# Three row blocks of the first batch transposed by DMA, and the turns behind the first batch set anew

## The chip, the cores and the metric

The kernel runs on one core of a Trainium2 chip. The metric is device time in microseconds. A core has TensorE (PE, with its weight loads PEld), VectorE (DVE), ScalarE (ACT), GpSimd (POOL), and SyncE (SP), which here only issues DMAs. Each of them works off its own instructions in order. Sixteen DMA engines move the data; the loads, the outputs and the DMA transposes are all issued on SP's queue, the MLP's weights on POOL's.

## The reference

Two stages run one after the other, on 4 batches, 8 heads, 768 positions and 64 channels a head. The first is a retention recurrence; the second mixes its output by a Fourier transform over positions and channels, normalizes, and applies an MLP of width 2048.

```python
for t in range(S):
    state = gamma[None, :, None, None] * state + einsum('bhd,bhe->bhde', k[:, :, t], v[:, :, t])
    y[:, :, t] = scale * einsum('bhd,bhde->bhe', q[:, :, t], state)
x = y.transpose(0, 2, 1, 3).reshape(B, S, H * D)          # 4 x 768 x 512
u = x + real(fft(fft(x, axis=1), axis=2))
un = (u - mean(u)) / sqrt(var(u) + 1e-6)                  # over the 512 channels
out = u + maximum(un @ w_ch1, 0) @ w_ch2
```

## The kernel before, in words

**Retention.** The 768 positions are cut into 6 chunks of 128, and the heads are taken in 4 pairs (called 0 to 3 in their order). For a pair, `cast_unit` turns the loaded float32 q, k and v into float16 on POOL (L428, L438, L443), `t_unit` makes the transposes qT and kT, `kv_unit` the chunk states (L683, L693), `a_unit` the scores inside the chunks (PE L664, then DVE's masked product L667), and `y_unit` the output (PE L714, L718, then ACT L726 into the tile x). For the second batch q and k are transposed on TensorE (L620), but kT of pairs 2 and 3 by DMA (L616). The third and fourth batch transpose both by DMA (L609, L611).

**Fourier mixing.** `fold_s`, `fold_d`, `fold_e` fold x by its symmetries on DVE, `s1_unit` is the transform over positions (L847), `s2_unit` that over channels, one row block of 128 positions at a time (PE L1009 or, for the first batch, L1025 and L1028; then ACT, DVE, and POOL L1037 and L1039, which write the tile u). `norm_unit` takes mean and variance on DVE (L1049, L1050) and writes the centred float16 row block `un` on ACT (L1051).

**MLP.** Each row block `un` is transposed into `unT` by `unT_unit`: either by four TensorE transposes into PSUM (L1074) and an eviction by DVE (L1076) or ACT (L1078), or by one DMA transpose on SP's queue (L1070). Before the change row blocks 3 to 5 of the second batch and all blocks of the third and fourth go by DMA; the first batch's and the second batch's blocks 0 to 2 go over TensorE. `h_unit` is the first matmul over 384 positions, in 16 units of four matmuls (L1087, evicted by ACT L1091 or DVE L1093); the first batch's first half is done by row block instead (`h0_unit`, L1104). `ch_unit` is the second matmul (L1130), in four parts of four matmuls for each row block, with the output's sum on DVE (L1134) and its DMA (L1138).

**Order.** The first batch's retention and mixing up to its third row block stand in a list written out by hand (`FIRST`), and every engine's order is pinned to it. Everything behind that is in streams: a stream is a list of units with a first and a last turn, and its units are spread evenly between the two (`emit`). One unit of turn is one batch of MLP: the first batch's MLP has 56 units in its "majors" stream, from turn 0 to 1, and the attention of batch b + 1 and the mixing run beside it. All units are emitted in the order of their turns. That order is a priority: a scheduler in the compiler then takes, on each engine, the unit that is ready and has the earliest turn, so units can be pulled forward where an engine would stand idle. Only POOL's order is kept as emitted (`pin`).

The turns that the change touches: `DM0` (first batch's row blocks 3 to 5: mixing between its first two numbers, transposes between its last two), `TS0` (second batch's casts and the five steps of its attention), `DA0` (second batch's transform over positions, then the mixing and transposes of its row blocks 0 to 2, counted from the end of the attention), `LD0` (the second batch's loads, L195) and `HT0` (`half_tables`, small tables for the folded transform, and `pad_unit`, zeros in the q tiles). The second batch's loads also wait for the seventh of the eight weight DMAs (`load_unit` with `after`), since both draw on the same DMA engines.

Of the kernel before, what the change touches and what calls it, by code (L numbers as in the profile page):

```python
# [12 lines left out]
ALU = mybir.AluOpType  # L13
# [44 lines left out]
ACT_ROWS = ((2, 5, 6, 7, 8, 9, 10, 14), (0, 3, 6, 7, 9, 10, 11, 12, 14, 15), (2, 4, 5, 6, 7, 8, 10, 11, 13, 14))  # L58


@with_exitstack
def kernel(
# [9 lines left out]
    nc = tc.nc  # L72
# [112 lines left out]
    def load_unit(b, i, after=None, names="qkv"):  # L185
        def run():
            h0 = 2 * PAIR_ORDER[i]
            for name in names:
                if (name, b, i) in in_of:
                    continue  # L190
                src = srcs[name]
                t = inp.tile([P, 2, NCH, D], f32, tag="in32", name=f"{name}32")
                rows = "h (p c) d -> p h c d" if b < NPE and name == "q" else \
# [13 lines left out]
                in_of[name, b, i] = t  # L207
        return run
# [34 lines left out]
    for h in range(H):  # L243
# [52 lines left out]
    def pad_unit():  # L296
        for j in range(2):
            nc.vector.memset(qzs[j][:, 0, :, D:P], 0.0)
            nc.vector.memset(qzs[j][:, 1, :, 0:D], 0.0)

# [115 lines left out]
    def cast_unit(b, i):  # L416
        def run():
            h0 = 2 * PAIR_ORDER[i]
            q32, k32, v32 = (in_of.pop((n, b, i)) for n in "qkv")
            kd = kp.tile([P, NCH, 2, D], f16, tag="kd16", name="kd16")  # L420
            v16 = vp.tile([P, NCH, 2, D], f16, tag="v16", name="v16")
            with ExitStack() as es:
                if b < NPE:
                    if (b, i - 1) in last_cast:
                        es.enter_context(tc.issue_after(last_cast[b, i - 1].ins))
                    q16 = qzs[i % 2].rearrange("p h c d -> p (h c d)")[
                        :, 0:NCH * P].rearrange("p (c h d) -> p c h d", c=NCH, h=2)
                    es.enter_context(tc.issue_after(nc.gpsimd.tensor_scalar(  # L428
                        out=q16, in0=q32.rearrange("p h c d -> p c h d"), scalar1=1.0,
                        scalar2=1.0, op0=ALU.mult, op1=ALU.mult).ins))  # L430
                else:
                    q16 = qzs[i % 2]
                    for h2 in range(2):
                        dst = q16[:, h2, :, D * h2:D * h2 + D]
                        nc.gpsimd.tensor_scalar(out=dst, in0=q32[:, h2], scalar1=1.0,
                                                scalar2=1.0, op0=ALU.mult, op1=ALU.mult)
                for h2 in range(2):
                    kc = nc.gpsimd.tensor_scalar(out=kd[:, :, h2, :], in0=k32[:, h2],  # L438
                                                 scalar1=gkd[:, h0 + h2:h0 + h2 + 1],
                                                 scalar2=1.0, op0=ALU.mult, op1=ALU.mult)  # L440
# [162 lines left out]
    def t_unit(b, i):  # L603
        def run():
# [9 lines left out]
            for dst, src in ((qT, q16_of[b, i]), (kT, kd_of[b, i])):  # L614
                if dst is kT and i in KD:
                    nc.sync.dma_start_transpose(kT, src.rearrange("p c h d -> p (c h d)"))  # L616
                    continue
                tq = ps_g.tile([P, NCH, P], f16, tag="g", name="tq", padded_shape=[P, 8, P])
                for c in range(NCH):
                    nc.tensor.transpose(tq[:, c, :], src[:, c].rearrange("p a b -> p (a b)"),  # L620
                                        ident16)
                if dst is qT:
                    for h2 in range(2 if b else 1):
                        rows = slice(D * h2, D * h2 + D) if b else slice(0, P)
                        dst = qT[rows, h2] if b else qT
                        (nc.scalar.copy if h2 == 0 or ON_ACT["q"][min(b, 2)] else nc.vector.tensor_copy)(
                            dst.rearrange("p c t -> p (c t)").rearrange(
                                "p (t c) -> p t c", c=NCH),
                            tq[rows].rearrange("p c t -> p t c"))
                else:  # L630
                    nc.scalar.copy(dst, tq)
# [434 lines left out]
    def unT_unit(b, kb):  # L1066
        def run():
            un, unT = lb[b].pop(("un", kb)), lb[b]["unT"]
            if b > 1 or b and kb >= 3:
                nc.sync.dma_start_transpose(unT[:, :, kb * P:(kb + 1) * P], un)  # L1070
                return
            pst = ps_g.tile([P, 4, P], f16, tag="g", name="pst", padded_shape=[P, 8, P])
# [84 lines left out]
    def attn_steps(b):  # L1157
        steps = []
        for step in range(6):
            un = []  # L1160
            if step < 4:
                un.append(held(cast_unit(b, step)))
            i = step - 1
            if 0 <= i < 4:
                un.append(kv_unit(b, i))
            i = step - 2
# [175 lines left out]
```

## Time and profile before

| | |
|---|---|
| median of 3 runs | 242.59 us (241.97 to 243.15) |
| the profiled execution's own time | 242.18 us |
| its span, first to last instruction | 240.4 us |
| granted TensorE clock | 1.00 |
| busy: PE, DVE, ACT, POOL | 228.3, 173.4, 120.8, 82.8 us |
| first matmul of the first batch's MLP (L1104) | 32.5 us |
| first h unit of its second half (L1087) | 60.3 us |
| first matmul of the second batch's MLP (L1087) | 91.0 us |

All times in the profile are of one execution, counted from its span's start. A line of a group reads: code line, engine, operation, what it writes and reads, how many, busy time, mean duration of one in ns, and the engine's idle time ahead of them with what ended it. In a timeline a line gives start, duration, engine, code line, operation and count, with neighbours of one kind merged; matmuls are pipelined, so a matmul's duration is longer than the step to the next one, and what a matmul costs is that step. "SPq" is SP issuing a DMA, and the time of an issue includes waiting for room in the queue.

### The profile page before, as it was taken

What the parts mean: (1) busy time and instruction counts of PE and PEld (TensorE: products, weight loads), DVE (VectorE), ACT (ScalarE), POOL (GpSimd) and SP (SyncE); (2) the same over time, 40 slices, a digit from 0 to 9 for tenths busy, and PEclk for the clock granted to TensorE, in tenths of its full rate; (3) what the DMA queues carried; (4) which work ended last, traced back from release to release, by engine and by line L of the source; (5) the groups of instructions that cost most, each with busy time, mean ns of one, the idle gap of its engine ahead of it and who ended that gap; (6) DMA issues with size and microseconds to landing.
All of it is one profiled execution on the core that took longest, in us unless ns stands there. A gap on an engine that the chain in (4) does not pass through costs nothing.

```text
span 240.4 us, 5243 instructions
## 1 busy us (share of the span) xinstructions
PE 228.3 (95%) x1999; PEld 142.5 (59%) x1999; DVE 173.4 (72%) x421; ACT 120.8 (50%) x268; POOL 82.8 (34%) x151
## 2 busy tenths in 40 slices
PE   0988999999999999999999999999999999999994
PEld 0466779766774756665567446655675455446542
DVE  8999887958898789977895749977886557215121
ACT  5989758675864544931148406722366227203400
POOL 7678802675300197840002808920004124000000
PEclk9999999999999999999999999999999999999999
DMA  7999999999999289979999488675100331221012
GB/s 181 231 271 238 236 206 208 215 248 246 260 215 230 47 197 218 179 144 146 256 277 208 103 174 213 131 109 153 46 0 0 90 109 24 43 90 45 0 44 87
DMA packets 100808, 36.77 MB, mean 153 GB/s; under 512 B 91440, under 2 KB 97840, under 8 KB 100784
## 3 DMA queue, kind: packets, MB, share of 16 engines
q1 hardware_dynamic: 96560, 32.25, 63.2%
q0 software_dynamic: 4224, 4.19, 10.5%
q8 instruction: 15, 0.25, 0.5%
q14 instruction: 9, 0.07, 0.1%
HBM read 27.26 MB, written 6.29 MB: 140 GB/s over the span
## 4 chain that ended last, share of the span: by engine, by line
PE 85%; DVE 4%; DMA 3%; POOL 2%; ACT 2%; SPq 1%; issue 1%; ACTq 0%
PE psc L1130 34%; PE psh L1087 28%; PE psh L1104 3%; PE wkA L664 3%; DMA v<-in_v_dram 3%; PE ps L847 3%; PE wkY L718 2%; PE pq L1009 2%; PE ps L827 1%; PE wkY L714 1%; PE wkK L683 1%; PE pq L921 1%; SPq L215 1%; PE tq L620 1%; POOL q16z L453 1%
## 5 line engine op out<-in xcount | busy, mean ns | idle before, releaser
L1130 PE MATMUL psc<-w,ht 128*128 128x512 f16 (+2 forms) x400 | 88.9, 370 | 0.0
L1087 PE MATMUL psh<-unT,w 128*128 128x384 f16 x448 | 81.6, 326 | 0.3 <-ACT ht L1091 0.3
L1130 PEld LDWEIGHTS <-ht 128*128 128x128 f16 x400 | 37.6, 98 | 36.7
L1087 PEld LDWEIGHTS <-w 128*128 128x128 f16 x448 | 42.1, 98 | 24.2 <-issue 0.8
L1091 ACT ACTIVATE ht<-psh 128x384 f16<-128x384 f32 x66 | 31.7, 490 | 41.2 <-PE psh L1087 40.6
L1037 POOL TENSOR_TENSOR u<-u,x 128x256 f32<-128x256 f32 x21 | 13.3, 635 | 107.8 <-DVE u L1016 95.6
L1134 DVE SCALAR_TENSOR_TENSOR ob<-psc,stats,u 128x512 f32<-128x512 f32 (+2 forms) x25 | 18.1, 725 | 29.2 <-PE psc L1130 29.0
L1093 DVE TENSOR_SCALAR ht<-psh 128x384 f16<-128x384 f32 x46 | 25.3, 550 | 8.9 <-PE psh L1087 8.4
L667 DVE TENSOR_TENSOR atm<-wkA,maskp 128x512 f16<-128x512 f32 x36 | 23.6, 681 | 1.5 <-PE wkA L664 1.5
L1051 ACT ACTIVATE un<-u,stats 128x512 f16<-128x512 f32 x21 | 14.9, 719 | 12.2 <-DVE stats L1050 8.2
L1049 DVE BATCH_NORM_STATS2 bst<-u 128x6 f32<-128x512 f32 x21 | 14.5, 688 | 4.9 <-POOL u L1039 4.7
L693 DVE SCALAR_TENSOR_TENSOR s<-s,gk,wkK 128x128 f16<-128x128 f16 x48 | 16.2, 337 | 2.4 <-ACT s L689 1.6
L726 ACT ACTIVATE x<-wkY,gexp 128x384 f16<-128x384 f32 x24 | 12.9, 581 | 9.0 <-PE wkY L718 8.9
L438 POOL TENSOR_SCALAR kd<-k,gexp 128x384 f16<-128x384 f32 x24 | 13.8, 586 | 3.3 <-DMA k<-in_k_dram 3.1
L664 PE MATMUL wkA<-qTz,kT 128*128 128x256 f16 x72 | 13.2, 272 | 0.1
L1039 POOL TENSOR_TENSOR u<-u,x 128x256 f32<-128x256 f32 x21 | 13.3, 635 | 0.0
L1011 ACT COPY qn<-pq 128x128 f32<-128x128 f32 x18 | 4.9, 274 | 13.7 <-PE pq L1009 13.7
L1104 PEld LDWEIGHTS <-w 128*128 128x128 f16 x192 | 11.0, 98 | 0.9 <-issue 0.6
L1104 PE MATMUL psh<-unT,w 128*128 128x128 f16 x192 | 11.4, 219 | 0.1
L1016 DVE SCALAR_TENSOR_TENSOR u<-pq,g,qn 128x256 f32<-128x256 f32 x18 | 8.5, 474 | 3.2 <-PE psh L1087 2.5
L443 POOL TENSOR_SCALAR v<-v 128x768 f16<-128x768 f32 x12 | 10.0, 832 | 1.6 <-DMA v<-in_v_dram 1.6
L664 PEld LDWEIGHTS <-kT 128*128 128x128 f16 x72 | 6.9, 98 | 5.7 <-issue 0.6
(177 smaller groups left out, 311.9 us busy)
## 6 DMA issues: line engine op xcount, KB each, us to landing
q<-in_q_dram SPq DMA_DIRECT2D x16, 384.0 KB, 6.1
k<-in_k_dram SPq DMA_DIRECT2D x16, 384.0 KB, 5.4
v<-in_v_dram SPq DMA_DIRECT2D x16, 384.0 KB, 6.0
out_dram<-ob SPq DMA_DIRECT2D x23, 256.0 KB, 2.4
w<-in_moe_w_ch_dram POOLq DMA_DIRECT2D x8, 512.0 KB, 10.9
unT<-un SPq DMA_TRANSPOSE x15, 2.4
out_dram<-ob SPq DMA_DIRECT2D x1, 192.0 KB, 1.9
kT<-kd SPq DMA_TRANSPOSE x10, 3.0
```

The source lines that it names most:

```text
L438: kc = nc.gpsimd.tensor_scalar(out=kd[:, :, h2, :], in0=k32[:, h2], scalar1=gkd[:, h0 + h2:h0 + h2 + 1], scalar2=1.0, op0=ALU.mult, op1=AL ...
L664: mm = nc.tensor.matmul(wk[:, c2], st["kT"][:, c, :], st["qT"][:, :, c, :], start=True, stop=True)
L667: nc.vector.tensor_tensor(out=st["atm"][:, 2 * part:2 * part + 2], in0=wk, in1=maskp[:, PAIR_ORDER[i]].unsqueeze(1).to_broadcast([P, 2, 2, ...
L693: nc.vector.scalar_tensor_tensor(out=s16[:, c], in0=s16[:, c - 1], scalar=gk2[:, hp:hp + 1], in1=wk[:, c - c0], op0=ALU.mult, op1=ALU.add)
L1049: nc.vector.bn_stats(bst, u[:, kb, :])
L1051: nc.scalar.activation(un, u[:, kb, :], AF.Identity, bias=stats[:, kb, 0:1], scale=-1.0)
L1087: nc.tensor.matmul(psh, w116[:, cb, fb * P:(fb + 1) * P], unT[:, cb, rt * 384:(rt + 1) * 384], start=(cb == 0), stop=(cb == 3))
L1091: nc.scalar.activation(ht16[:, fb, :], psh, AF.Relu, bias=0.0, scale=-1.0)
L1093: nc.vector.tensor_scalar(out=ht16[:, fb, :], in0=psh, scalar1=-1.0, scalar2=0.0, op0=ALU.mult, op1=ALU.max)
L1104: mm = nc.tensor.matmul(psh[:, f], w116[:, cb, fb * P:(fb + 1) * P], unT[:, cb, kb * P:(kb + 1) * P], start=(cb == 0), stop=(cb == 3))
L1130: nc.tensor.matmul(psc[:, c0:c1], ht16[:, fb, rb3 * P:(rb3 + 1) * P], w216[:, fb, c0:c1], start=(fb == 0), stop=(fb == NFB - 1))
L1134: nc.vector.scalar_tensor_tensor(out=ob[:, c0:c1], in0=psc[:, c0:c1], scalar=lb[b]["st"][:, rb, 3:4], in1=lb[b]["u"][:, rb, c0:c1], op0=AL ...
```

## The change

Row blocks 3, 4 and 5 of the first batch are transposed by a DMA on SP's queue in place of TensorE and an eviction; the table `UD` says which blocks of the first two batches do so. All turns of the streams behind the first batch's list, up to the second batch's first three row blocks, get new numbers. `QD`, a way to transpose q by DMA as well, is added but empty, so what it guards is as before.

```diff
-DM0, DM1 = (0.183, 0.205, 0.286, 0.408), (0.004, 0.137, 0.232, 0.341)
-TS0 = (0.228, 0.358, 0.398, 0.465, 0.512, 0.573, 0.684, 0.694)
+DM0, DM1 = (0.079, 0.166, 0.238, 0.282), (0.004, 0.137, 0.232, 0.341)
+TS0 = (0.335, 0.390, 0.418, 0.440, 0.525, 0.605, 0.703, 0.726)
 TS1 = (-0.040, -0.020, 0.048, 0.585)
-DA0, DA1 = (0.043, 0.161, 0.176, 0.190, 0.284, 0.321), (0.063, 0.067, 0.063, 0.158, 0.168, 0.189)
-LD0, LD1 = (0.223, 0.312), (-0.370, 0.140)
-HT0 = (0.666, 0.693, 0.632, 0.590)
+DA0, DA1 = (0.013, 0.146, 0.137, 0.188, 0.260, 0.288), (0.063, 0.067, 0.063, 0.158, 0.168, 0.189)
+LD0, LD1 = (0.142, 0.375), (-0.370, 0.140)
+HT0 = (0.712, 0.769, 0.606, 0.689)
 NPE = 2
 KD = (2, 3)
+QD = ()
 NT = 0.6
+UD = ((3,4,5), (3, 4, 5))
...
             un, unT = lb[b].pop(("un", kb)), lb[b]["unT"]
-            if b > 1 or b and kb >= 3:
+            if b > 1 or kb in UD[b]:
                 nc.sync.dma_start_transpose(unT[:, :, kb * P:(kb + 1) * P], un)
                 return
```

Turns of some units before and after:

| unit | before | after |
|---|---|---|
| mixing of the first batch's blocks 3, 4, 5 | 0.190, 0.198, 0.205 | 0.108, 0.137, 0.166 |
| their transposes | 0.327, 0.367, 0.408 | 0.253, 0.267, 0.282 |
| second batch's loads, pairs 0 to 3 | 0.245, 0.268, 0.290, 0.312 | 0.200, 0.259, 0.317, 0.375 |
| its casts, pairs 0 to 3 | 0.293, 0.409, 0.472, 0.521 | 0.363, 0.422, 0.452, 0.536 |
| scores of pair 2 (three parts) | 0.556 to 0.573 | 0.582 to 0.605 |
| y of pair 3 | 0.686 | 0.707 |
| second batch's transform over positions | 0.766 to 0.855 | 0.772 to 0.872 |
| its mixing of blocks 0, 1, 2 | 0.875, 0.879, 0.884 | 0.880, 0.897, 0.914 |
| their transposes | 0.990, 1.003, 1.015 | 0.995, 1.005, 1.014 |

More of the change, by code (lines that the diff above doesn't have):

```diff
@@ L192, in run @@
                 t = inp.tile([P, 2, NCH, D], f32, tag="in32", name=f"{name}32")
-                rows = "h (p c) d -> p h c d" if b < NPE and name == "q" else \
+                rows = "h (p c) d -> p h c d" if b < NPE and name == "q" and i not in QD else \
                     "h (c p) d -> p h c d"
@@ L294, in half_tables, with pad_unit @@
                                 scalar2=1.0, op0=ALU.mult, op1=ALU.mult)
-    def pad_unit():
-        for j in range(2):
+    def pad_unit(js=None):
+        for j in (js if js is not None else {0, 1} - {i % 2 for i in QD}):
             nc.vector.memset(qzs[j][:, 0, :, D:P], 0.0)
@@ L422, in run @@
             with ExitStack() as es:
-                if b < NPE:
-                    if (b, i - 1) in last_cast:
-                        es.enter_context(tc.issue_after(last_cast[b, i - 1].ins))
+                if b < NPE and (b, i - 1) in last_cast:
+                    es.enter_context(tc.issue_after(last_cast[b, i - 1].ins))
+                if b < NPE and i not in QD:
                     q16 = qzs[i % 2].rearrange("p h c d -> p (h c d)")[
@@ L616, in run @@
                     nc.sync.dma_start_transpose(kT, src.rearrange("p c h d -> p (c h d)"))
+                    continue
+                if dst is qT and i in QD:
+                    nc.sync.dma_start_transpose(qT.rearrange("p h c t -> p (h c) t"),
+                                                src.rearrange("p h c d -> p (h c d)"))
                     continue
@@ L1161, in attn_steps @@
             if step < 4:
+                if b == 1 and step in QD:
+                    un.append(lambda j=step % 2: pad_unit([j]))
                 un.append(held(cast_unit(b, step)))
```

6 lines of the change are left out of this document (4 added, 2 removed).

## The prediction

> **What bounds the kernel now.** I read the page's busy shares and its chain first, then the windows, the tile views of the transposes, the timelines and the waits of the stage that is changed.
>
> ```profile
> PE 228.3 (95%) x1999; PEld 142.5 (59%) x1999; DVE 173.4 (72%) x421; ACT 120.8 (50%) x268; POOL 82.8 (34%) x151
> PE 85%; DVE 4%; DMA 3%; POOL 2%; ACT 2%; SPq 1%; issue 1%; ACTq 0%
> ```
>
> TensorE is busy for 95% of the span and carries 85% of the chain. Time is won here only by taking work off TensorE or by closing its few gaps. The windows (PE, PEld, DVE, ACT, POOL, then clock, DMA share, GB/s) show this in the stage that is changed:
>
> ```profile
> 44.00:48.00 4.00, 4.00 (x42) 2.67 (x40) 3.65 (x11) 3.05 (x5) 2.64 (x5) 1.00 1.10 235
> 56.00:60.00 4.00, 4.00 (x49) 2.66 (x47) 3.28 (x7) 2.33 (x5) 2.07 (x3) 1.00 1.22 249
> 72.00:76.00 4.00, 4.00 (x34) 2.11 (x33) 3.14 (x7) 2.49 (x7) 0.00 (x0) 1.00 1.17 236
> ```
>
> PE is full, the granted clock is 1.00, and the DMA engines are full too (share above 1). So a transpose taken off PE frees time there and costs time in a stream that is already saturated. The tile view of the PSUM tile of the transposes, and the line view of the DMA transposes that later batches use already:
>
> ```profile
> L1074 PE MATMUL pst<-ident,un x32: 219/219/219, 35.3 to 90.1; 128*128 128x128 f16 x32
> L1076 DVE COPY unT<-pst x4: 411/416/426, 37.4 to 90.5; 128x512 f16<-128x512 f16 x4
> L1078 ACT COPY unT<-pst x4: 564/579/586, 38.7 to 90.1; 128x512 f16<-128x512 f16 x4
> ...
> L1070 SPq DMA_TRANSPOSE unT<-un x15: 1188/1216/2628, 98.5 to 204.8; - x15
> ...
> DMA to landing us min/median/max: 2.3/2.4/4.8
> ```
>
> The PE timeline shows what a row block's four transposes hold up, and the first use of the third pair's kT:
>
> ```profile
> 48.08 0.39 PE L1074 MATMUL pst<-ident,un 128*128 128x128 f16 x4
> 48.31 1.89 PE L1130 MATMUL psc<-w,ht 128*128 128x512 f16 x8
> ...
> 63.91 2.11 PE L1087 MATMUL psh<-unT,w 128*128 128x384 f16 x12
> 65.86 0.82 PE L664 MATMUL wkA<-qTz,kT 128*128 128x256 f16 x6
> ```
>
> The next matmul starts 0.23 us after the four. Of SP's and POOL's timelines, the end of the second batch's loads:
>
> ```profile
> 56.33 4.16 SPq L1138 DMA_DIRECT2D out_dram<-ob  x3
> 60.65 1.35 SPq L616 DMA_TRANSPOSE kT<-kd  x1
> ...
> 58.92 0.83 POOL L428 TENSOR_SCALAR q16z<-q 128x768 f16<-128x768 f32 x1 [1.17 <-DMA q<-in_q_dram]
> 60.56 1.15 POOL L438 TENSOR_SCALAR kd<-k,gexp 128x384 f16<-128x384 f32 x2 [0.82 <-DMA k<-in_k_dram]
> ```
>
> The casts wait for loads that land some 1.7 us apart (46.9 for the first k to 61.6 for the last v, ten loads). The third pair's kT is issued behind three outputs at 60.65 and lands at 64.47.
>
> **Transposes off TensorE.** Three row blocks (3, 4, 5) by four transposes. The price is the step to the next instruction, not the row's 219 ns: 0.224 us for four, so 3 x 0.224 = **-0.67 us** on the path, as PE has no gap at these places. ACT loses two evictions (2 x 0.58) and DVE one (0.42); neither is on the path there (both idle over a microsecond between 50 and 54), so nothing. The Trainium skill, TensorE: Matmul & The Clock Gate, Part 4, gives about 275 ns for such a transpose inside a kernel. By that, as an estimate, twelve would free 3.3 us; the trace's 56 ns steps decide against it.
>
> **Three DMA transposes on SP.** Each takes 1.2 us of SP's time and 2.4 us to land, 4.8 at worst. The last `un` (block 5) is written on ACT by 47.2, its first user is the second half's first matmul at 60.27, 0.67 earlier after the change: even behind a full stream, at the loads' 6.1 us, it lands by about 55. Nothing on the path. What they delay is the queue behind them: the loads of pairs 2 and 3 (L195), the outputs (L1138) and the kT transposes (L616). In the DMA stream a block is 128 KB where a load is 384 KB per 1.7 us, so 0.57 us each, 1.7 in all. SP's own time bounds it from above, 3 x 1.2 = 3.6 us, if nothing of it overlaps; the lower bound is nothing. I take 1.7, since SP already waits for room in its queue there (a load's issue takes 0.4 to 2.4 us). Slack on the other side: pair 3's q cast is done at 59.8 and transposed at 63.6 (3.8 us), its v cast at 62.5 and used at 66.5 (4.0): covered. The third pair's kT has 65.86 - 64.47 = 1.4 us, the thinnest cover.
>
> **Turns set anew.** One turn is from 32.5 to 91.0 us, 58.5 us; one unit of the 56 is 0.018. They decide who goes first among what is ready, so half_tables and pad (already pulled to DVE's free time at 47.6 to 50.7) stay free, as do the batch's own mix units: their PE part already runs at 36.9 in a gap, and POOL keeps its order. Load 3 now stands behind the first output (turn 0.375 against 0.339), 0.65 us of stream at the spacing at which the outputs land; pair 3's 3.8 us cover it. The second batch's casts and attention move later by 0.01 to 0.07; its third pair's scores go behind one more h unit (0.65 us), so they are due at 65.86 + 0.65 - 0.67 = 65.8, and kT, 1.7 us late, lands at 66.2: 0.3 us, which a ready h unit hides if the order has one there, as it has now (two of them go ahead of the scores). I take 0. In the stage's gaps,
>
> ```profile
> PE ps L891 <- DVE xg L882: 0.2, 1, 0.2
> ```
>
> is the only one that counts as a wait; all steps lengthened by over 60 ns between 35 and 91 us come to 1.3 us. I see no reason why the new turns close them all or open others: between -1.3 and the prices below, I take 0.
>
> **Sum.** The profiled execution took 242.18 us (span 240.4 and 1.8 around it): 242.18 - 0.67 = 241.5. It lies 0.41 under the median 242.59 of the three runs; against the median, 242.59 - 0.67 = **241.9 us**, by itself too little to be told from no change (0.5%, 1.2 us, is about what can be told).
>
> **Rivals.** (1) The new turns also close the gaps: up to 1.3 us more, 240.6 to 241.3. For it: the waits of the second batch's y units on DVE's score products sit among what is moved. Against: they come from DVE, which is solid from 65.4 to 74.1, and little leaves it.
>
> (2) Slower: the third pair's kT comes late. Place: L664's wait for L616. With SP's whole 3.6 us, kT lands at 68.1, PE, due at 65.8, stands 2.3 us: 242.59 - 0.67 + 2.3 = 244.2. It decides for slower from a stall of 1.9 us, kT landing after 67.7, 3.2 us later than now. For it: SP is a queue in order, an output now stands ahead of the last load, and each transpose waits there for its `un`. Against: the stream's own price is half of that, and h units can go first.
>
> (3) The seam to the second batch eats the gain. The chain of waits around it:
>
> ```profile
> 74.41 1.06 ACT x L726 x2
> ...
> 89.84 0.45 PE pst L1074 x8
> 90.28 0.23 PE pq L1009 x4
> 90.51 0.28 PE wkK L683 x5
> 90.79 0.33 PE pq L1009 x4
> 91.13 3.95 PE psh L1087 x24
> ```
>
> From the last y (74.4) through folds, DFT and norm to the new unT it takes 16.7 us; meanwhile PE works off the first batch's rest and, at its end, 0.8 us of pulled-forward work. The two arrive together. If the chain does not start earlier, PE's 0.67 us turns into waiting: 242.6. If the last y comes later as its turn says (0.686 to 0.707, 1.2 us), 243.8. Against: DVE has 0.7 us of outputs between the last norms' steps that another order can put behind them.
>
> (4) A transpose costs its whole row: 12 x 0.219 = 2.6 us, 240.0. The timeline's steps speak against it. It is the trace's nearest to the page's 275 ns.
>
> **How the numbers follow.** The forecast, 241.4 to 242.6, 0.36. Rival 1: 0.20. Rival 2: 0.28, of which 0.22 beyond its point. Rival 3: 0.14, of which 0.04 slower by over 0.5% (a little behind 243.8). Rival 4: 0.02. Faster 0.20 + 0.02 = 0.22; same 0.36 + 0.06 + 0.10 = 0.52; slower 0.22 + 0.04 = 0.26. The predicted time is the forecast's, 241.9; the range goes from rival 1's end, 240.6, to rival 2's, 244.3.
>
> **What would show it.** L1074 with 20 matmuls in place of 32 and L1070 with 18 issues; PE's work before the first matmul of the second batch's h units less by 0.67 us. That matmul at 90.3 means the forecast, at 91.0 rival 3, later than 91.5 a new stall. A wait of L664 for kT, with L616 landing after 66.5, is rival 2; casts waiting for loads after 64 us would mean that the stream is delayed by more than 1.7 us. A gap ahead of L1087 near 59 to 60 us, released by a DMA, would mean that the transposes themselves come late, which I left out. The stage after 91 us should be as long as before; if it isn't, the later batches' loads were pushed, and the forecast is wrong there.

## The result, and the profile after

The changed kernel takes 243.96 us (median of six runs, 243.67 to 244.56) against 242.33 us for the kernel before in the same comparison (six runs, 241.97 to 243.15): a ratio of **1.0066, 95% interval 1.0044 to 1.0088**. It is slower by 1.6 us. The profiled execution took 244.01 us, its span is 242.0 us, 1.6 us longer than before. The forecast was 241.9 us and "no change". The time lies inside the range given, near its upper end, but not by the mechanism that put that end there.

The page's busy shares and chain of the changed kernel:

```profile
PE 227.3 (94%) x1987; PEld 141.6 (59%) x1987; DVE 173.6 (72%) x420; ACT 119.7 (49%) x266; POOL 82.9 (34%) x151
...
PE 78%; DVE 6%; DMA 6%; POOL 3%; ACT 3%; issue 2%; SPq 1%; ACTq 0%; DVEq 0%
```

TensorE has twelve matmuls and 1.0 us of work less, as meant, and yet the span is longer. The chain says where to look: TensorE's share of it fell from 85% to 78%, and that of DMA rose from 3% to 6%. The tile views of the transposes (code lines have moved: L1074 is now L1082, L1070 is L1078) show the change itself:

```profile
L1082 PE MATMUL pst<-ident,un x20: 219/219/230, 35.7 to 90.4; 128*128 128x128 f16 x20
```

```profile
L1078 SPq DMA_TRANSPOSE unT<-un x18: 1189/1216/2137, 45.1 to 206.6; - x18
...
DMA to landing us min/median/max: 2.3/2.4/4.8
```

And of the table of waits of the changed kernel (engine, tile, line, what it waited for: total us, times, longest):

```profile
PE wkA L672 <- DMA qTz<-q16z: 1.5, 1, 1.5
...
PE pst L1082 <- ACT un L1059: 0.3, 1, 0.3
```

Neither is in the table of before. The second is at the seam to the second batch; the first is far behind everything that the change touches. The span cut into stages shows the same (us; a stage goes from one first matmul to the next, the batches' ones being those of their h units):

| stage | before | after | difference |
|---|---|---|---|
| start to the first batch's MLP (L1104, now L1112) | 32.50 | 32.90 | +0.40 |
| from there to the second batch's MLP | 58.52 | 58.43 | -0.09 |
| second batch's MLP to the third's | 51.28 | 52.77 | **+1.49** |
| third to fourth | 51.68 | 51.66 | -0.02 |
| fourth to the end | 46.40 | 46.25 | -0.15 |

The 0.40 us of the first row are not the change's: over the fourteen profiles of this study, whose list for the first batch is one and the same, it took between 32.45 and 33.03 us, whichever kernel it was. So two things need an explanation: the 0.67 us taken off TensorE brought 0.09 in their own stage, and the stage behind, in which no turn was changed, lost 1.49 us.

**The stage behind.** There the third batch's last pair waits for its qT. TensorE's timeline in the changed kernel, and then the chain of waits around it (start, duration, what):

```profile
113.81 2.54 PE L1138 MATMUL psc<-w,ht 128*128 128x512 f16 x11
117.83 0.38 PE L672 MATMUL wkA<-qTz,kT 128*128 128x256 f16 x2 [1.48 <-DMA qTz<-q16z]
```

```profile
110.98 6.71 DMA qTz<-q16z
117.70 0.14 issue
117.83 0.38 PE wkA L672 x2
```

Counted as steps from one matmul to the next, TensorE loses 1.65 us here. In the kernel before it lost 0.30 at the same matmul. TensorE reaches these scores 24.85 us behind the second batch's first h unit in both kernels; the transposed q lands 25.02 us behind that unit before the change, and 26.37 us after it. SP's timeline shows the order in which it is issued. Before:

```profile
92.86 0.43 SPq L195 DMA_DIRECT2D k<-in_k_dram  x1
...
97.95 0.39 SPq L195 DMA_DIRECT2D v<-in_v_dram  x1
98.45 2.63 SPq L1070 DMA_TRANSPOSE unT<-un  x1
101.40 1.21 SPq L611 DMA_TRANSPOSE kT<-kd  x1
102.66 1.51 SPq L609 DMA_TRANSPOSE qTz<-q16z  x1
104.27 2.82 SPq L1070 DMA_TRANSPOSE unT<-un  x2
107.26 1.21 SPq L611 DMA_TRANSPOSE kT<-kd  x1
108.52 0.57 SPq L195 DMA_DIRECT2D q<-in_q_dram  x1
109.19 4.14 SPq L609 DMA_TRANSPOSE qTz<-q16z  x1
```

And after:

```profile
93.26 0.43 SPq L197 DMA_DIRECT2D q<-in_q_dram  x1
...
97.78 0.57 SPq L197 DMA_DIRECT2D k<-in_k_dram  x1
98.40 0.71 SPq L197 DMA_DIRECT2D v<-in_v_dram  x1
101.74 1.42 SPq L615 DMA_TRANSPOSE kT<-kd  x1
103.20 1.49 SPq L613 DMA_TRANSPOSE qTz<-q16z  x1
104.79 4.15 SPq L1078 DMA_TRANSPOSE unT<-un  x3
109.04 1.23 SPq L615 DMA_TRANSPOSE kT<-kd  x1
110.32 0.57 SPq L197 DMA_DIRECT2D q<-in_q_dram  x1
110.98 2.67 SPq L613 DMA_TRANSPOSE qTz<-q16z  x1
```

The same transfers stand in another order. Before, the third batch's last q load went out ahead of all of this (at 83.82), and one of the second batch's unT transposes filled the time that SP spent waiting for the casts. After, that q load comes at 93.26, the k and v loads behind it side by side at 97.78 and 98.40, SP stands idle from 99.1 to 101.7, and all three unT transposes come behind kT and qT of the third pair. So the issue of the last qT begins 1.47 us later behind the second batch's first h unit (19.65 against 18.18), and it lands 1.35 us later. SP is done with that issue 22.3 us behind the unit in both kernels, so its later start alone doesn't make the landing late. That the landing hangs on SP's order is what the runs below show; by which step it does is not shown.

**The changed stage.** I count each of TensorE's steps at the usual step of its shape (0.16 us for 384 columns, 0.215 for 512), and what a step has above that as loss. From the first batch's first MLP matmul to the second batch's, the usual steps come to 55.38 us before and 54.74 after, 0.64 less; the losses come to 3.14 before and 3.69 after, 0.55 more. Almost all of the latter is one wait, at 90.27, for the centred row block of the second batch:

```profile
89.55 0.40 PE L1082 MATMUL pst<-ident,un 128*128 128x128 f16 x4
90.27 0.40 PE L1082 MATMUL pst<-ident,un 128*128 128x128 f16 x4 [0.33 <-ACT un L1059]
```

The last y of the second batch ends 42.44 us behind the stage's start (41.93 before), its last `un` 57.31 (56.89). Why that y is later can be counted. Ahead of the third pair's scores TensorE takes 20 matmuls of h units, where it took 12 before:

```profile
64.30 3.41 PE L1095 MATMUL psh<-unT,w 128*128 128x384 f16 x20
67.55 0.82 PE L672 MATMUL wkA<-qTz,kT 128*128 128x256 f16 x6
```

With these eight, 63 of the 64 h matmuls of the first batch's second half stand ahead of the last y, where 55 did. Eight steps are 1.3 us more ahead of it, the twelve transposes 0.64 less, and the y comes 0.51 later. From its end to the second batch's first h unit it takes 15.99 us (16.58 before, when nine h matmuls were left for that stretch; now one is). So what came off TensorE ahead of the y was more than filled by work pulled forward, and the chain behind the y came later.

### The profile page after: what moved, and what is told of

It reads as the page before. It is cut to its first block, busy times and chain, and to the rows that moved or that the text cites. A ratio compares the mean times of both kernels' runs of the same rounds, so it can differ in the third digit from the quotient of the medians.

```text
span 242.0 us, 5220 instructions
## 1 busy us (share of the span) xinstructions
PE 227.3 (94%) x1987; PEld 141.6 (59%) x1987; DVE 173.6 (72%) x420; ACT 119.7 (49%) x266; POOL 82.9 (34%) x151
## 4 chain that ended last, share of the span: by engine, by line
PE 78%; DVE 6%; DMA 6%; POOL 3%; ACT 3%; issue 2%; SPq 1%; ACTq 0%; DVEq 0%
PE psc L1138 29%; PE psh L1095 29%; PE psh L1112 3%; PE wkA L672 3%; DMA v<-in_v_dram 3%; DMA qTz<-q16z 3%; PE ps L855 3%; PE wkY L726 2%; PE pq L1017 1%; PE wkY L722 1%; PE wkK L691 1%; SPq L217 1%; PE ps L835 1%; PE tq L628 1%; POOL u L1047 1%
## 5 line engine op out<-in xcount | busy, mean ns | idle before, releaser
L1112 PEld LDWEIGHTS <-w 128*128 128x128 f16 x192 | 11.0, 98 | 0.8 <-issue 0.5
L1112 PE MATMUL psh<-unT,w 128*128 128x128 f16 x192 | 11.4, 219 | 0.1
```

What stands on the lines that cost most here:

```text
L1112: mm = nc.tensor.matmul(psh[:, f], w116[:, cb, fb * P:(fb + 1) * P], unT[:, cb, kb * P:(kb + 1) * P], start=(cb == 0), stop=(cb == 3))
```

## The experiments

In the edits, `order on SP` is a dependency that only fixes the order of two DMAs on SP's queue: the first argument is issued behind the second. No semaphore and no wait is added. In the changed kernel and in its four runs that reorder only the entries on SP near the second and third batch, the orders on TensorE, VectorE, ScalarE and GpSimd are the same, instruction by instruction; so they are in the kernel before and its two such runs. The experiments of the last part and those with other turns have orders of their own. "Stage A" is from the first batch's first MLP matmul to the second batch's (58.52 us before, 58.43 after), "stage B" from there to the third batch's (51.28 and 52.77). A stage, a wait or a landing is that of the one execution profiled; four of these took 0.8 to 1.6 us more than the median of their run (the DMA transposes alone, unT and the q load both moved, the earlier kT, the old DM0), so their waits may be longer than usual.

### One half of the change at a time

Only the DMA transposes, all turns as before:

```diff
+UD = ((3,4,5), (3, 4, 5))
...
-            if b > 1 or b and kb >= 3:
+            if b > 1 or kb in UD[b]:
```

> The old turns with the three DMA transposes alone. Theory (SP's order in the second batch): the change's 1.6 us come from one transpose of the second batch (row block 3) that now stands behind the third batch's transposes of pair 2 on SP; here it stands ahead of them again, so TensorE's wait ahead of the last pair's scores (L672) should be 0.3 us as in the kernel before and the time 241.7 to 242.5 us. Rival (the DMA transposes themselves cost): about 243.9 us, as in the changed kernel.

Measured: 246.81 us (246.34 to 247.83), ratio 1.0173 (1.0149 to 1.0197). Stage A takes 64.38 us, stage B 51.14. SP's timeline and TensorE's waits:

```profile
55.35 1.48 SPq L197 DMA_DIRECT2D v<-in_v_dram  x1
56.92 4.29 SPq L1078 DMA_TRANSPOSE unT<-un  x1
61.31 0.52 SPq L1146 DMA_DIRECT2D out_dram<-ob  x1
61.92 2.53 SPq L1078 DMA_TRANSPOSE unT<-un  x2
```

```profile
PE psh L1095 <- DMA unT<-un: 3.0, 1, 3.0
PE wkY L722 <- ACT qTz L634: 0.6, 1, 0.6
```

Neither of the expected times came. With the old turns the transposes stand behind all of the second batch's loads, land at 63.1, 64.4 and 65.7 us, and the second half of the MLP waits until 65.85. The step that the prediction put at nothing is worth over 3 us when its cover is gone. And there is no wait at the third batch's last qT (it lands 24.52 us behind the second batch's first h unit): the DMA transposes by themselves do not cause it.

Only the new turns, all transposes of the first batch on TensorE, as an edit to the changed kernel:

```diff
-UD = ((3,4,5), (3, 4, 5))
+UD = ((), (3, 4, 5))
```

> The new turns with all of the first batch's transposes on TensorE. Theory (SP's order in the second batch): row block 3's transpose stands ahead as in the kernel before, so a wait of 0.3 us at L672 and 242.0 to 242.9 us. Rival (the new turns alone are slow, whatever is transposed where): 243.5 us or more, 0.67 us above the changed kernel if TensorE's transposes cost as before.

Measured: 243.58 us, ratio 1.0043 (1.0029 to 1.0058). Stage A takes 59.78 us, stage B 51.57. TensorE's waits:

```profile
PE pst L1082 <- ACT un L1059: 1.0, 2, 0.8
...
PE wkA L672 <- DMA qTz<-q16z: 0.4, 1, 0.4
```

The rival's time, 243.5 us or more, held. The new turns alone cost 0.4%, most of it in the changed stage. The TensorE transposes now come ahead of their `un` (a step loss of 0.98 us at 46.80), the seam has a wait of 0.40 us with or without DMA transposes, and the third batch's last qT is late by 0.57 us. The halves do not add up (1.7% and 0.4% against 0.7%): the turns are made for the DMA transposes.

### Which part of SP's order makes the last qT late

Three orders, each with the unT transpose of the second batch's row block 3 moved. First the changed kernel with that transpose ahead of the third pair's kT, as before the change:

```diff
-                nc.sync.dma_start_transpose(unT[:, :, kb * P:(kb + 1) * P], un)
+                x = nc.sync.dma_start_transpose(unT[:, :, kb * P:(kb + 1) * P], un).ins
+                if (b, kb) == (1, 3):
+                    tc.add_manual_dep(sp_of["k", 2, 2], x.name, mybir.DependencyInfo(mybir.DependencyClass.NoSync, mybir.DependencyReason.DATA), reason="order on SP")
```

> The changed kernel with one edge: the third batch's kT of pair 2 is issued behind the second batch's row block 3 on SP, as in the kernel before. Theory (SP's order): the wait at L672 falls from 1.65 to about 0.3 us, the stage from the second to the third batch's first h unit from 52.8 to 51.4 us, the time to 242.3 to 242.7 us. Rivals (transposes or turns in the first batch): no change, 243.9 us.

Measured: 243.58 us, ratio 1.0045 (1.0029 to 1.0062). The step loss falls from 1.65 to 1.24 us only. The moved transpose holds SP for 3.73 us, as it is issued directly behind the k and v loads (2.63 us in the kernel before, which has the k load earlier).

Then the kernel before, with the same transpose behind the third pair's kT and qT, as after the change:

```diff
+                if (b, kb) == (1, 3):
+                    tc.add_manual_dep(x, sp_of["k", 2, 2].name, mybir.DependencyInfo(mybir.DependencyClass.NoSync, mybir.DependencyReason.DATA), reason="order on SP")
+                    tc.add_manual_dep(x, sp_of["q", 2, 2].name, mybir.DependencyInfo(mybir.DependencyClass.NoSync, mybir.DependencyReason.DATA), reason="order on SP")
```

> The kernel before with the opposite edge: the second batch's row block 3 is transposed behind the third batch's kT and qT of pair 2 on SP, as in the changed kernel. Theory (SP's order): SP reaches the last qT 1.25 us later, the wait ahead of the last pair's scores (L664) grows from 0.3 to some 1.5 us, the time to 243.4 to 243.9 us. Rivals: no change, 242.3 us.

Measured: 243.08 us, ratio 1.0033 (1.0015 to 1.0051). The loss rises from 0.30 to 0.79 us: half a microsecond, less than the 1.2 expected, by an edit to the kernel before that touches nothing of the first batch. Both runs say that this transpose's place is a part of the cause, worth 0.4 to 0.5 us, and that there is more.

Last, the changed kernel with that and with the third batch's last q load ahead of its first qT:

```diff
+                if (name, b, i) == ("q", 2, 3):
+                    tc.add_manual_dep(sp_of["q", 2, 0], dma.ins.name, mybir.DependencyInfo(mybir.DependencyClass.NoSync, mybir.DependencyReason.DATA), reason="order on SP")
```

> The changed kernel with both shifts on SP undone: the third batch's last q load is issued ahead of its first qT (as in the kernel before), and the second batch's row block 3 is transposed ahead of the third batch's pair 2. Undoing the second alone left a wait of 1.24 us. Theory (what is left is the load that had moved into the seam, 384 KB in the same stream): the last qT lands about 25.0 to 25.3 us after the second batch's first h unit, as before, the wait is 0.2 to 0.5 us, the time 242.3 to 242.8 us. Rival (the seam is slow for another reason, such as the second batch's later loads): the wait stays at 1.2 us or more, 243.5 us.

Measured: 243.24 us (242.24 to 245.05), ratio 1.0043 (1.0016 to 1.0069), and a loss of 1.88 us in an execution of 244.43; the 0.2 to 0.5 expected was missed. The k and v loads still stood side by side (97.52 and 98.14), and the transpose behind them held SP for 4.15 us. Moving single entries did not bring the order of before back.

### The load ahead of the last qT

In both kernels the fourth batch's first q load is issued just ahead of the late qT. It is wanted much later. Behind it:

```diff
+                if (b, i) == (3, 0):
+                    tc.add_manual_dep(dma.ins, sp_of["q", 2, 3].name, mybir.DependencyInfo(mybir.DependencyClass.NoSync, mybir.DependencyReason.DATA), reason="order on SP")
```

In the changed kernel:

> The changed kernel with one edit: the fourth batch's first q load is issued on SP behind the third batch's last qT (in the kernel it stands directly ahead of it). Theory (the 1.65 us wait is the landing of that qT, and the load ahead of it is part of the price): a qT behind no load lands some 3.8 us after its issue in place of 6.7 us, so it is there 3 us earlier, the wait at L672 is gone, the stage from the second to the third batch's first h unit is 51.1 us and the time 242.1 to 242.5 us. Rival (the wait is set by something else than this landing, such as the cast or TensorE's own use of the buffer): 243.9 us.

Measured: 242.19 us, before 242.34, ratio 0.9998 (0.9980 to 1.0016). The wait is gone, stage B takes 51.14 us. SP and TensorE there:

```profile
109.17 1.23 SPq L618 DMA_TRANSPOSE kT<-kd  x1
110.49 1.30 SPq L615 DMA_TRANSPOSE qTz<-q16z  x1
111.84 1.02 SPq L197 DMA_DIRECT2D q<-in_q_dram  x1
```

```profile
113.61 2.75 PE L1142 MATMUL psc<-w,ht 128*128 128x512 f16 x12
116.20 0.38 PE L676 MATMUL wkA<-qTz,kT 128*128 128x256 f16 x2
```

The transpose lands 5.4 us behind its issue in place of 6.7, and no longer waits 0.66 us for the load's issue. One moved load takes the whole loss away; the rest of SP's order is that of the changed kernel.

In the kernel before, the same edit:

> The kernel before with the same edit (the fourth batch's first q load behind the third batch's last qT). Theory: its 0.3 us wait at L664 goes, 241.9 to 242.3 us, at most 0.2% faster. Rival (the load is needed early, in the fourth batch): a new wait in the third stage, slower than 242.6 us.

Measured: 241.89 us, ratio 0.998 (0.997 to 0.999). The 0.30 us that the kernel before lost here go too. This version is the fastest of the study and beats both kernels, by little.

### SP's order of before, with the change otherwise whole

The changed kernel, with the order on SP behind the first batch set to that of before, entry by entry (the last q and k load of the third batch, the second pair's qT ahead of its kT, the third pair's the other way, and unT as above), the late q load left where it is in both:

```diff
+                if (name, b, i) == ("q", 2, 3):
+                    tc.add_manual_dep(sp_of["q", 2, 0], dma.ins.name, mybir.DependencyInfo(mybir.DependencyClass.NoSync, mybir.DependencyReason.DATA), reason="order on SP")
+                if (name, b, i) == ("k", 2, 3):
+                    tc.add_manual_dep(sp_of["q", 2, 1], dma.ins.name, mybir.DependencyInfo(mybir.DependencyClass.NoSync, mybir.DependencyReason.DATA), reason="order on SP")
...
+                if (b, i) == (2, 1):
+                    tc.add_manual_dep(sp_of["k", b, i], sp_of["q", b, i].name, mybir.DependencyInfo(mybir.DependencyClass.NoSync, mybir.DependencyReason.DATA), reason="order on SP")
+                if (b, i) == (2, 2):
+                    tc.add_manual_dep(sp_of["q", b, i], sp_of["k", b, i].name, mybir.DependencyInfo(mybir.DependencyClass.NoSync, mybir.DependencyReason.DATA), reason="order on SP")
```

> The changed kernel with SP's order at the second batch made the same as in the kernel before, from the third batch's first qT to its last: the last q load ahead of the first qT, the last k load ahead of the second qT (in the run before this one it stood with the last v load right ahead of the transposes), row block 3 of the second batch, then kT and qT of pair 2. All other engines as in the changed kernel. Theory (the order of these loads and transposes on SP, and nothing else, makes the wait): the last qT lands 25.0 to 25.3 us after the second batch's first h unit, the wait at L672 is 0.2 to 0.5 us, the stage 51.2 to 51.5 us, the time 242.3 to 242.8 us. Rival (something of the first batch's stage reaches over, such as later loads of the third batch): the wait stays above 1 us, 243.4 us or more.

Measured: 242.08 us (241.79 to 243.49), ratio 0.9992 (0.9977 to 1.0007). Stage A takes 58.42 us, stage B 51.16. SP's timeline there:

```profile
98.04 0.57 SPq L197 DMA_DIRECT2D v<-in_v_dram  x1
98.71 2.54 SPq L1088 DMA_TRANSPOSE unT<-un  x1
101.54 1.21 SPq L620 DMA_TRANSPOSE kT<-kd  x1
102.81 1.34 SPq L617 DMA_TRANSPOSE qTz<-q16z  x1
```

The qT lands 24.35 us behind the second batch's first h unit, ahead of the 24.85 at which it is wanted. The orders of the other engines are those of the changed kernel. So the order on SP makes the whole slowdown, and the rest of the change comes out at no difference. The expectation was off by one thing: SP's order is now that of the kernel before, yet the qT lands 0.67 us earlier behind the unit than there, so no wait of 0.2 to 0.5 us is left. Why it is earlier is open. Against the run with unT and the q load moved, this one adds only the third batch's last k load ahead of its second pair's transposes and the third pair's kT ahead of its qT, and the loss goes from 1.88 us to none, the median from 243.24 to 242.08. So the larger part lies with the k load, which had stood beside the v load, or with the order of that pair; no run tells the two apart.

### The transposes ahead of the loads, with the old turns

If the DMA transposes only needed to be early, an order on SP would do in place of new turns. The kernel with the DMA transposes and all old turns, with the q load of pair 2 behind the three transposes:

```diff
+                if (name, b, i) == ("q", 1, 2):
+                    q12.append(dma.ins)
...
-                nc.sync.dma_start_transpose(unT[:, :, kb * P:(kb + 1) * P], un)
+                x = nc.sync.dma_start_transpose(unT[:, :, kb * P:(kb + 1) * P], un).ins
+                if b == 0:
+                    tc.add_manual_dep(q12[0], x.name, mybir.DependencyInfo(mybir.DependencyClass.NoSync, mybir.DependencyReason.DATA), reason="order on SP")
```

> The old turns with the three DMA transposes, and these issued ahead of pair 2's loads on SP (alone, with the old turns, they stood behind all loads, landed at 63 to 66 us, and TensorE stood still for over 4 us ahead of the first batch's second half). Theory (where they stand on SP decides): that wait is gone, from the first row block to the second batch's first h unit 58.3 to 58.8 us in place of 64.4. SP's order at the second batch comes out as in the changed kernel, so its wait there stays at 1.3 to 1.9 us: 243.6 to 244.2 us in all. Rival (the DMA transposes need the new turns on the other engines as well): over 245 us.

Measured: 246.81 us, ratio 1.0178 (1.0147 to 1.0209), as the rival had it. The three transposes and the output that stands among them take SP from 49.61 to 55.30, so the loads of pair 2 begin at 55.30 (47.97 in the kernel before). TensorE then waits 1.15 us for a cast of q and 0.59 for one of v, and 1.53 us for the third batch's last qT. (A wait of 1.04 us at 36.57 for a weight load lies ahead of the edit.) Early transposes alone move the loss from the transposes to the loads; the casts and the attention behind the loads have to be set later with them, which is what the new turns do.

### What sets the seam

With the late qT out of the way, three runs asked where TensorE's 0.67 us went in stage A. All of them have the fourth batch's q load behind, and compare with that run's 242.19 us, its stage A of 58.81 us and its 0.49 us of wait for `un`.

The third pair's kT ahead of the first batch's second and third output on SP:

```diff
+                    if i == 2:
+                        for o in outs0:
+                            tc.add_manual_dep(o, x.name, mybir.DependencyInfo(mybir.DependencyClass.NoSync, mybir.DependencyReason.DATA), reason="order on SP")
```

> The changed kernel with the fourth batch's first q load behind the third batch's last qT (the run that took the 1.65 us wait away), and the second batch's kT of pair 2 ahead of the first batch's second and third outputs on SP. Theory for the first batch's stage (TensorE's 0.67 us are lost at the seam, since the second batch's chain starts later: kT of pair 2 lands 2.3 us later than before, the last y 0.5 us later, un 0.4 us later, and TensorE then waits 0.5 us for un): kT lands 0.7 to 1.3 us earlier, the last y 0.3 to 0.5 us earlier, the wait for un falls below 0.25 us, the stage from the first row block to the second batch's first h unit is 57.9 to 58.2 us, the time 241.6 to 242.0 us. Rival (the seam is set by VectorE's work or by the new turns, not by kT): the stage stays at 58.4 to 58.8 us, 242.2 us.

Measured: 242.69 us, ratio 1.0019 (1.0002 to 1.0037); stage A 59.10 us. The kT lands 34.05 us behind the stage's start instead of 35.14, but the last y stays at 42.41 (42.80 in the run it compares with), the last `un` comes at 57.98 (57.69), and TensorE, which now takes the scores earlier, meets new waits of 0.56 us for kT and 0.30 for a cast. So an earlier kT alone does not bring the seam forward. It does change TensorE's order: 11 h matmuls in a row stand ahead of the scores in place of 20, and 57 ahead of the last y in place of 63; but the new waits take what that gives, and the way from the y to the last `un` takes 15.57 us in place of 14.89.

The casts' and the attention's turns (TS0) as before the change:

```diff
-TS0 = (0.335, 0.390, 0.418, 0.440, 0.525, 0.605, 0.703, 0.726)
+TS0 = (0.228, 0.358, 0.398, 0.465, 0.512, 0.573, 0.684, 0.694)
```

> The changed kernel with the fourth batch's first q load behind the third batch's last qT, and the second batch's casts and attention (TS0) back at their old turns. Theory: the wait of 0.4 to 0.5 us for un ahead of the second batch's first h unit comes from the last y of the second batch, which stands later by its new turn (42.4 us behind the first matmul of the first batch's MLP, against 41.9 before). With the old turns the last y is back at 41.9 or earlier, the wait falls under 0.2 us, from the first matmul of the MLP to that h unit it takes 58.0 to 58.2 us in place of 58.4 to 58.8, and the time is 0.5 us under that of the changed kernel with the q load behind (242.2): 241.7 us, 0.997 to 0.998 of the time before. Rival (the wait comes from the new turns of the mixing and the transforms, DA0): the wait for un stays over 0.35 us, the stretch stays at 58.4 us or more, and the time at 242.2. Rival (old casts' turns with new loads' turns starve POOL): a wait for a cast of 0.5 us or more between 58 and 70 us, and a time over 242.6.

Measured: 243.30 us (243.03 to 243.46), ratio 1.0042 (1.0028 to 1.0055); stage A 59.18 us, stage B 51.79. My theory fell, and clearly: with the earlier turns the last y comes later (43.18 us), not earlier. TensorE meets a wait of 0.50 us for a q cast at 63.47 and two for `un` of 0.36 and 0.50 at the end. That is the third expectation's wait; the time that it named, over 242.6, held too. Stage B is 0.65 us longer than in the run it compares with, and 0.37 of it is work of TensorE's that had there been done ahead of the seam. The casts' new, later turns fit loads that stand later behind the DMA transposes.

The first batch's own mixing and transposes (DM0) as before the change:

```diff
-DM0, DM1 = (0.079, 0.166, 0.238, 0.282), (0.004, 0.137, 0.232, 0.341)
+DM0, DM1 = (0.183, 0.205, 0.286, 0.408), (0.004, 0.137, 0.232, 0.341)
```

> The changed kernel with the fourth batch's first q load behind the third batch's last qT, and the first batch's own mixing and DMA transposes of row blocks 3 to 5 (DM0) back at their old, later turns. Theory (the seam is set by the second batch's chain, which these turns do not touch): the wait for un ahead of the second batch's first h unit stays between 0.3 and 0.6 us, from the first matmul of the MLP to that unit it takes 58.4 to 58.9 us, and the time is 242.1 to 242.4. Rival (the transposes, later, stand behind the second batch's loads on SP): the second half's first matmul waits for a DMA transpose near 61 us by 0.5 us or more, and the time is over 242.7. Rival (the earlier mixing took DVE from the second batch, so its late turn brings the chain forward): the last y at 42.0 us or less behind the MLP's first matmul, no wait for un over 0.2 us, 241.7.

Measured: 247.29 us (246.71 to 249.20), ratio 1.0214 (1.0184 to 1.0245); stage A 65.57 us. The first rival held, and its price was over 242.7 by far. The transposes land at 59.3, 60.2 and 66.7 us, and TensorE waits for two things in a row:

```profile
64.08 0.57 PE L632 MATMUL tq<-ident,q16z 128*128 128x128 f16 x6 [1.84 <-POOL q16z L432]
66.72 1.76 PE L1099 MATMUL psh<-unT,w 128*128 128x384 f16 x5 [2.08 <-DMA unT<-un]
```

The earlier turns of mixing and transposes are what makes the DMA transposes cheap at all.

| run | time, us | ratio | stage A | stage B | loss at the last qT |
|---|---|---|---|---|---|
| before | 242.33 | | 58.52 | 51.28 | 0.30 |
| changed | 243.96 | 1.0066 | 58.43 | 52.77 | 1.65 |
| changed, SP's order of before | 242.08 | 0.9992 | 58.42 | 51.16 | none |
| changed, q load behind | 242.19 | 0.9998 | 58.81 | 51.14 | none |
| before, q load behind | 241.89 | 0.998 | 58.50 | 50.97 | none |

## Why the prediction was wrong

**Transposes off TensorE: right.** 20 matmuls in place of 32, 1.0 us less busy time, and 0.64 us less of TensorE's usual steps where 0.67 was forecast from the steps of 56 ns. Rival 4, the whole row of 219 ns each, is out.

**Three DMA transposes on SP: right in their own stage.** They land at 49.3, 53.4 and 53.8 us ("by about 55"), and their first user at 59.79 does not wait. The working named no price for the loss of that cover; the runs with the old turns (all of them, or DM0 alone) did: 3.2 and 2.3 us of wait, because there the last of the three stands behind all of the second batch's loads. They were hidden by the new turns, not by the slack of before, which I had used.

**The delay behind them: sized right, wrongly taken as free.** The third pair's kT lands 2.33 us later behind the stage's start; 1.7 for the transposes and 0.65 for the load behind the output make 2.35. (With the new turns alone it lands 0.83 later, so the shares are nearer 1.5 and 0.83.) It landed at 67.21, past the 66.5 that I had named as the mark of rival 2, and in this profile nobody waited, as TensorE took 20 matmuls of h units ahead of the scores in place of 12 (three units of four, where I had read two). The cover was thin: in three of the four runs that share this stage's orders kT landed at 67.44 to 67.75 and TensorE waited 0.25 to 0.42 us, so rival 2's wait was there, at up to 0.42 us of the 2.3 that I had priced. And the cover was not free. I wrote that "a ready h unit hides" the delay and took 0; the eight matmuls pulled forward are the ones that put the last y, and with it the seam, later. The casts of pair 3 came 3.1 us later, more than the 1.7 that I allowed, and their slack of 3.8 and 4.0 us held.

**Turns set anew at nothing: this step failed, in two ways.** For the changed stage I saw no reason for a new gap. There was one, 0.49 us for `un` at the seam, and with smaller ones it took nearly all of the 0.64 us: rival 3 as it was priced, with TensorE's gain turned into waiting (first h unit at 91.33, which is 90.93 without the late start, where rival 3 said 91.0 and the forecast 90.3). And I let the effect of the new turns end with that stage: "The stage after 91 us should be as long as before". It became 1.49 us longer. No turn in it had changed, but the scheduler's order of SP's entries had, and a transpose that already stood at its limit (0.30 us late in the kernel before) came 1.35 us later. Setting SP's order back takes it all away: 0.9992.

Rival 2 had the right kind of mechanism, a transposed tile late on a queue in order with TensorE's scores waiting for it, and the wrong place: the third batch's last qT at 117 us, not the second batch's third kT at 66. It also had the wrong cause. It is not the three added transposes as such that delay it (they landed by 53.8 us, and with the old turns alone that qT comes in time), but another order of the same entries. That order comes out anew with each edit: with the old turns and the transposes ahead of the loads, row block 3's transpose again stands behind the third pair's, and the wait is 1.53 us. The range's upper end is given as 244.3; rival 2's own sum makes 244.2.

**What was in the profile.** The kernel before showed the mark: 4.14 us of issue and 6.8 us to landing for that qT, against 1.5 and 3.7 for its like, and a step of 0.30 us too long at 116.16. I read the waits and the gaps of the changed stage only, so a queue at its limit 25 us behind it went unread.

**What stays open.** The seam is accounted for by counting and not by an edit. In six of the nine kernels with the new DA0 it takes 15.99 to 16.01 us from the end of the last y to the second batch's first h unit, whether the y comes 42.42 or 43.18 us into the stage; what makes the y late differs from run to run. Whether the old DA0 would shorten these 16 us was not tried. That TensorE's order pulls eight h matmuls forward because kT stands later on SP is suggested by the run with kT moved ahead, which has six of them back, and by the new turns alone, which pull none; no run gives TensorE its old order with the rest of the change. Nor is it shown why the scheduler's order of SP differs; that it moved entries because its view of what is ready when had moved is only argued.

## What to carry to other kernels

Where a scheduler orders the queues, a change to one stage's turns can reorder a DMA queue in a later stage that was not touched: compare the order of every queue over the whole span, and look in the profile of before for entries that already land at their deadline. Put a load that is wanted late behind a transpose that is wanted now; here that one line was worth 0.2% on the old kernel and the whole loss on the new one. Work taken off the busiest engine shows up only if the chain that feeds its next stage comes earlier too, and work pulled forward to cover a late tile can push that chain back.

## What the runs showed of the hardware

**A transpose behind a load.** The transpose of q in the third batch's last pair, with a 384 KB load issued just ahead of it, lands 6.7 to 6.8 us behind its issue (110.98 to 117.70 after, 109.19 to 116.03 before) and 6.0 to 7.1 us in the seven other runs that have the load there. In the five with the load behind it, it took 3.8 to 5.5 us, where the median of the eight transposes of q is 3.7 to 3.8. The Trainium skill, DMA: Bandwidth & Descriptors, section "Issuing engines are not separate DMA queues", holds that spreading DMAs over issuing engines saves only the issuing time, which is usually small beside the DMA itself. Here it is not small: a transpose of a row block takes 1.2 us of SP's time and lands in 2.4, and the 4.2 us that three of them take stand between the third pair's qT and the fourth's kT. No run here issued them from another engine.

**A stall slows TensorE after it ends.** In the run with the DMA transposes and the old turns, TensorE stood for 3.0 us ahead of 65.85. Its windows (PE, PEld, DVE, ACT, POOL, then the granted clock):

```profile
62.00:65.85 3.85, 0.86 (x25) 0.71 (x22) 1.40 (x5) 2.52 (x4) 1.43 (x3) 0.77 0.63 165
65.85:68.00 2.15, 2.15 (x7) 0.99 (x8) 0.00 (x0) 0.49 (x1) 0.00 (x0) 0.50 1.02 287
...
70.50:73.00 2.50, 2.50 (x21) 1.73 (x20) 1.68 (x4) 0.76 (x2) 0.00 (x0) 0.93 1.30 253
```

The granted clock is 0.50 for about 5 us, in which matmuls of 384 columns step by 0.32 us instead of 0.16. Sixteen of those steps cost 2.5 us more: nearly as much again as the stall. In the run with the old DM0, TensorE stood for 1.84 us ahead of 64.08 and, after 0.6 us of work, for 2.08 us ahead of 66.72:

```profile
62.20:64.35 2.15, 0.31 (x7) 0.28 (x6) 0.32 (x2) 1.06 (x2) 0.83 (x1) 1.00 1.31 250
64.40:66.70 2.30, 0.25 (x4) 0.09 (x2) 0.71 (x3) 1.58 (x2) 1.69 (x3) 0.50 1.18 251
66.70:69.00 2.30, 2.28 (x8) 1.10 (x8) 0.00 (x0) 0.49 (x1) 0.29 (x1) 0.50 0.95 227
```

The clock is 1.00 up to 64.35 and 0.50 from 64.40: it fell just behind the first stand, before the second began. The Trainium skill, TensorE: Matmul & The Clock Gate, section "Why this matters for your kernels", tells to leave no idle gap of over about 3 us between bursts, or the clock falls to half. The first run's stand of 3.0 us is at that limit, though the clock there had fallen at 64.05, 1.2 us into it. In the second a stand of 1.84 us was enough, with two waits of 0.44 and 0.22 us in the 2 us ahead of it. The waits of 1.65 and 1.88 us at the last qT left the clock at 1.00.
